# Two grouped-query attention blocks: scores computed transposed, exponentials written straight as P^T, sums by a ones-matmul, and one order by hand that mixes attention with the projections

## The chip, the cores and the metric

The kernel runs on one core of one Trainium2 chip. The metric is device microseconds of one launch. The engines are TensorE (PE, with its weight loads shown as PEld), VectorE (DVE), ScalarE (ACT), GpSimd (POOL) and the DMA queues, of which SyncE's (SP) is the main one here. Matrices are bf16, accumulation in PSUM is fp32.

## The reference

Two independent problems, A and B, of the same shape; the outputs stand side by side.

```
x [16, 32, 1024]   k_cache, v_cache [16, 4, 512, 128]   wq [1024, 4096]   wo [4096, 1024]
q = x @ wq                       -> [16 batches, 32 heads, 32 rows, 128]
k, v: each of the 4 kv heads serves 8 query heads
p = softmax(q k^T / sqrt(128))   -> rows of 512
o = p v
out = o (heads joined) @ wo      -> [16, 32, 1024];  concatenate A and B on the last axis
```

A *group* below is one batch and one kv head: 8 heads x 32 rows = 256 query rows against 512 keys. There are 64 groups in a problem and 128 in all.

## The kernel before

Everything is laid out so that the contracted index lies on the 128 partitions. x is transposed on TensorE (L123) into `xT`. `q_projection` makes 32 heads per problem, each 8 matmuls of 512 columns (L145), evacuated with the scale 1/sqrt(128) on ACT (L92) and DVE (L97) by turns. `attention` then walks over batches and kv heads. For one group:

- two matmuls of 512 columns give the scores, query rows on the partitions (L189, `s_ps`);
- DVE takes the negated row maximum (L197, `nmx`), ACT the exponential of each half with that bias, which also accumulates the row sums (L203, `p_sb`, `rs`);
- DVE inverts the sums (L211), POOL multiplies the probabilities by them (L214);
- eight 128x128 transposes on TensorE turn P into P^T (L222, `pT_ps`), and DVE copies it to SBUF (L228, `pT`);
- four matmuls of 256 columns with V as weights give the output (L231, `o_ps`), and ACT copies it into `oT` (L238).

`o_projection` makes 32 tiles of 128x256 per problem, each 32 matmuls of 256 columns (L254, `f_ps`), evacuates them (L90, L95) and sends them out (L264). K arrives by a transposing DMA of 1 MB per two batches (L170, `kT`, two buffers), V by 512 KB per batch (L178, three buffers), wq in 512 KB and wo in 2 MB pieces (L139, L248). All of them are issued from SP's queue, so a transfer that waits for its buffer holds back those behind it.

The order of instructions on each engine is set by the framework's scheduler from the priorities of the program's order, with a few order-only links; it puts B's q projection into A's attention, and most of A's output projection into B's attention.

Of the kernel before, what the change touches and what calls it, by code (L numbers as in the profile page):

```python
# [9 lines left out]
FP32 = mybir.dt.float32  # L11
ACTF = mybir.ActivationFunctionType
# [3 lines left out]
P = 128  # L16
# [5 lines left out]
SCALE = float(DH) ** -0.5  # L22


@with_exitstack
def kernel(
# [16 lines left out]
    _, _, SK, _ = A_k_cache.shape  # L43
# [5 lines left out]
    WH = 2  # L49
    OCW = 256  # L50
    NOC = NOUT // OCW
    KB = 2

    out_flat = out.flatten_outer_dims()

    const = ctx.enter_context(tc.tile_pool(name="const", bufs=1))
    xpool = ctx.enter_context(tc.tile_pool(name="xpool", bufs=1))
    wqpool = ctx.enter_context(tc.tile_pool(name="wqpool", bufs=6))
    wopool = ctx.enter_context(tc.tile_pool(name="wopool", bufs=2))
    qopool = ctx.enter_context(tc.tile_pool(name="qopool", bufs=3))  # L60
    ktpool = ctx.enter_context(tc.tile_pool(name="ktpool", bufs=2))
    vpool = ctx.enter_context(tc.tile_pool(name="vpool", bufs=3))
    work = ctx.enter_context(tc.tile_pool(name="work", bufs=3))
    small = ctx.enter_context(tc.tile_pool(name="small", bufs=4))
    outpool = ctx.enter_context(tc.tile_pool(name="outpool", bufs=3))
    psum = ctx.enter_context(
        tc.tile_pool(name="psum", bufs=1, space=bass.MemoryType.PSUM)
    )

    ident = const.tile([P, P], BF16, name="ident")  # L70
    make_identity(nc, ident[:])

# [5 lines left out]
    ORDER_ONLY = mybir.DependencyInfo(mybir.DependencyClass.NoSync, mybir.DependencyReason.DATA)  # L78

    def after(inst, first, why):  # L80
        if first is not None and inst is not None:
            tc.add_manual_dep(inst.ins, first.ins.name, ORDER_ONLY, reason=why)

    evac_toggle = [0]

    def _evac(out_ap, in_ap, scale):
        evac_toggle[0] ^= 1
        if evac_toggle[0]:
            if scale is None:
                nc.scalar.copy(out=out_ap, in_=in_ap)  # L90
            else:
                nc.scalar.mul(out=out_ap, in_=in_ap, mul=scale)  # L92
        else:
            if scale is None:
                nc.vector.tensor_copy(out=out_ap, in_=in_ap)  # L95
            else:
                nc.vector.tensor_scalar_mul(out=out_ap, in0=in_ap, scalar1=scale)  # L97
# [215 lines left out]
```

## Time and profile before

| | |
|---|---|
| median of 3 runs | 436.87 us (436.11 to 437.38) |
| span of the profiled execution, first to last instruction | 433.9 us (the page gives no other time of its own; the median is 2.97 us above this span) |
| TensorE busy | 418.8 us, 97% of the span, granted clock 1.00 |
| VectorE busy | 279.5 us, 64% |
| ScalarE busy | 256.4 us, 59% |
| GpSimd busy | 176.4 us, 41% |
| DMA | 71.89 MB, SP's queue at 74.8% of 16 engines' time |

Read it by stages: up to about 70 us there is q projection of A alone, to about 208 us attention of A with q projection of B, then a short stretch of q projection, to about 355 us attention of B with output projection of A, and then output projection alone. A busy share is an average over these. A row of instructions gives the count, the busy time of their union and the mean length of one; since matmuls overlap in the array, the mean length is a latency, and the pace comes from counts in a window of one kind of work. Some matmul records are missing from the trace (494 of 512 of the q projection are there).

### The profile page before, as it was taken

Reading aid. Unit: us, or ns where it says so; the run is one execution under the profiler, and the core shown is the slowest. Engines: PE = TensorE matmul, PEld = TensorE weight load, DVE = VectorE, ACT = ScalarE, POOL = GpSimd, SP = SyncE. Lnnn points to the kernel's source line nnn. Section 1 sums busy time; section 2 is a strip of 40 time slices with the busy share of each in tenths; the row PEclk is TensorE's granted clock in tenths of the full one; section 3 lists DMA queues with packets and bytes.
Section 4 is the critical chain, followed back from the end, with each engine's and each line's share of the span. In section 5 each row is a group of like instructions: output and inputs, shape, how many; then the busy total and the mean of one; then the engine's idle time right before and its main releaser. Section 6 shows DMA issues by size and latency. Waiting matters only on the chain.

```text
span 433.9 us, 8980 instructions
## 1 busy us (share of the span) xinstructions
PE 418.8 (97%) x3343; PEld 280.7 (65%) x3392; DVE 279.5 (64%) x564; ACT 256.4 (59%) x693; POOL 176.4 (41%) x262
## 2 busy tenths in 40 slices
PE   3999999999999999999999999999999999999997
PEld 2544444665666666566566766667667678888886
DVE  0122214999999999999269999999999950000000
ACT  2121113888888888888259888998988850000000
POOL 0000001566666666666126666666666640000000
PEclk9999999999999999999999999999999999999999
DMA  8945699797596999995566595995579007458800
GB/s 273 261 144 145 163 257 272 177 201 166 137 234 134 158 207 269 221 185 108 130 173 109 120 184 118 268 204 111 122 165 274 12 8 185 137 132 211 213 20 18
DMA packets 204076, 71.89 MB, mean 166 GB/s; under 512 B 133376, under 2 KB 203008, under 8 KB 204032
## 3 DMA queue, kind: packets, MB, share of 16 engines
q1 hardware_dynamic: 204032, 71.31, 74.8%
q8 instruction: 26, 0.43, 0.4%
q14 instruction: 18, 0.15, 0.1%
HBM read 52.43 MB, written 2.10 MB: 126 GB/s over the span
## 4 chain that ended last, share of the span: by engine, by line
PE 90%; DVE 3%; issue 2%; POOL 2%; DMA 1%; SPq 1%; DVEq 0%; POOLq 0%
PE f_ps L254 26%; PE q_ps L145 25%; PE pT_ps L222 16%; PE o_ps L231 14%; PE s_ps L189 10%; POOL p_sb L214 2%; DMA wq_sb<-in_A_wq_dram 1%; DVE nmx L197 1%; SPq L111 1%; DVE pT L228 1%; PE xT_ps L123 1%; DVE qT L97 0%; DVE rr L211 0%; DVE o_sb L95 0%; DVEq L95 0%
## 5 line engine op out<-in xcount | busy, mean ns | idle before, releaser
L214 POOL TENSOR_SCALAR p_sb<-p_sb,rr 128x512 bf16<-128x512 bf16 x256 | 175.7, 692 | 177.2 <-DVE rr L211 126.5
L203 ACT ACTIVATE p_sb<-s_ps,nmx 128x512 bf16<-128x512 f32 x256 | 173.9, 685 | 27.8 <-DVE nmx L197 12.4
L197 DVE TENSOR_REDUCE nmx<-s_ps 128x2 f32<-128x1024 f32 x128 | 154.4, 1207 | 0.5 <-PE s_ps L189 0.5
L254 PE MATMUL f_ps<-wo_sb,oT 128*128 128x256 bf16 x1024 | 123.1, 273 | 1.0
L254 PEld LDWEIGHTS <-oT 128*128 128x128 bf16 x1024 | 99.9, 98 | 24.3
L228 DVE COPY pT<-pT_ps 128x1024 bf16<-128x1024 bf16 x128 | 88.3, 690 | 12.2 <-PE pT_ps L222 4.9
L222 PE MATMUL pT_ps<-ident,p_sb 128*128 128x128 bf16 x1024 | 93.2, 220 | 1.9 <-POOL p_sb L214 0.6
L145 PEld LDWEIGHTS <-wq_sb 128*128 128x128 bf16 x512 | 50.0, 99 | 60.7 <-DMA wq_sb<-in_A_wq_dram 2.2
L222 PEld LDWEIGHTS <-p_sb 128*128 128x128 bf16 x1024 | 68.0, 98 | 21.8 <-POOL p_sb L214 14.1
L231 PE MATMUL o_ps<-pT,v_sb 128*128 128x256 bf16 x512 | 77.3, 273 | 0.2
L189 PE MATMUL s_ps<-kT,qT 128*128 128x512 bf16 x225 | 69.1, 379 | 0.3 <-ACT p_sb L203 0.2
L145 PE MATMUL q_ps<-xT_b,wq_sb 128*128 128x512 bf16 x244 | 63.9, 379 | 1.2
L231 PEld LDWEIGHTS <-v_sb 128*128 128x128 bf16 x512 | 43.1, 97 | 33.4 <-DVE pT L228 18.6
L145 PE MATMUL q_ps<-xT,wq_sb 128*128 128x512 bf16 x250 | 57.3, 387 | 2.3 <-DMA wq_sb<-in_A_wq_dram 2.0
L238 ACT CAST oT<-o_ps 128x256 bf16<-128x256 f32 x128 | 47.8, 373 | 15.2 <-PE o_ps L231 11.5
L97 DVE TENSOR_SCALAR qT<-q_ps 128x512 bf16<-128x512 f32 x32 | 22.1, 689 | 52.6 <-PE q_ps L145 52.6
L95 DVE CAST o_sb<-f_ps 128x256 bf16<-128x256 f32 x16 | 6.8, 422 | 70.9 <-PE f_ps L254 70.9
L92 ACT ACTIVATE qT<-q_ps 128x512 bf16<-128x512 f32 x32 | 19.1, 596 | 54.7 <-PE q_ps L145 51.9
L203 ACT ACTIVATION_READ_ACCUMULATOR p_sb<-s_ps,nmx 128x1 f32 x256 | 50.9, 199 | 0.0
L90 ACT CAST o_sb<-f_ps 128x256 bf16<-128x256 f32 x16 | 5.9, 371 | 66.8 <-PE f_ps L254 66.8
L211 DVE RECIPROCAL rr<-rs 128x1 f32<-128x1 f32 x256 | 36.6, 153 | 2.1 <-ACT p_sb L203 2.0
L189 PEld LDWEIGHTS <-qT 128*128 128x128 bf16 x256 | 20.1, 98 | 2.2 <-issue 0.9
(13 smaller groups left out, 21.0 us busy)
## 6 DMA issues: line engine op xcount, KB each, us to landing
wq_sb<-in_A_wq_dram SPq DMA_DIRECT2D x16, 512.0 KB, 4.2
v_sb<-in_A_v_cache_dram SPq DMA_DIRECT2D x16, 512.0 KB, 5.1
wq_sb<-in_B_wq_dram SPq DMA_DIRECT2D x16, 512.0 KB, 5.4
wo_sb<-in_A_wo_dram SPq DMA_DIRECT2D x4, 2048.0 KB, 9.7
v_sb<-in_B_v_cache_dram SPq DMA_DIRECT2D x16, 512.0 KB, 4.1
wo_sb<-in_B_wo_dram SPq DMA_DIRECT2D x4, 2048.0 KB, 9.3
out_dram<-o_sb SPq DMA_DIRECT2D x32, 64.0 KB, 2.3
x_sb<-in_A_x_dram SPq DMA_DIRECT2D x4, 256.0 KB, 3.2
```

Of the source, the lines that this page charges most:

```text
L97: nc.vector.tensor_scalar_mul(out=out_ap, in0=in_ap, scalar1=scale)
L145: nc.tensor.matmul(q_ps[:], lhsT=wq_sb[:, dc, hl * DH:(hl + 1) * DH], rhs=xT[:, dc, :], start=(dc == 0), stop=(dc == DC - 1),)
L189: sm = nc.tensor.matmul(s_ps[:, half, :], lhsT=qT[:, b, h0:h0 + HALF, :].rearrange("p h s -> p (h s)"), rhs=kT[:, bl, g, :], start=True, s ...
L197: nc.vector.tensor_reduce(out=nmx[:], in_=s_ps[:], axis=AX.X, op=ALU.max, negate=True)
L203: nc.scalar.activation(out=p_sb[:, half, :], in_=s_ps[:, half, :], func=ACTF.Exp, bias=nmx[:, half:half + 1], scale=1.0, accum_out=rs[:, h ...
L211: rc = nc.vector.reciprocal(out=rr[:, half:half + 1], in_=rs[:, half:half + 1])
L214: nc.gpsimd.tensor_scalar(out=pn[:, half, :], in0=p_sb[:, half, :], scalar1=rr[:, half:half + 1], scalar2=1.0, op0=ALU.mult, op1=ALU.mult,)
L222: nc.tensor.transpose(pT_ps[:, kc, half * P:(half + 1) * P], pn[:, half, kc * P:(kc + 1) * P], ident[:],)
L228: prev_pT_evac = nc.vector.tensor_copy(out=pT[:], in_=pT_ps[:])
L231: nc.tensor.matmul(o_ps[:], lhsT=v_sb[:, g, kc, :], rhs=pT[:, kc, :], start=(kc == 0), stop=(kc == KC - 1),)
L238: nc.scalar.copy(out=oT[:, g * REP:(g + 1) * REP, b * SQ:(b + 1) * SQ], in_=o_ps[:].rearrange("p (h s) -> p h s", s=SQ),)
L254: nc.tensor.matmul(f_ps[:], lhsT=oT[:, h, tt * P:(tt + 1) * P], rhs=wo_sb[:, h, :], start=(h == 0), stop=(h == HQ - 1),)
```

## The change

The whole program is rewritten in one function, `fast_path`, with a hand-written order (no scheduler), and a second function, `general_path`, that holds a plain version of the kernel before and is entered only behind a branch.

- **Transposed scores.** K^T is the weight and q the moving operand: for each group four matmuls of 256 columns give the scores with the keys on the partitions (`scores`, L350). The keys are taken with a step of 4 in K^T, so that partition p of piece c holds key 4p+c, and V is loaded to match, which makes its rows in a partition consecutive.
- **Exponential straight to P^T.** One ACT instruction of 1024 columns with a fixed shift of 44 and the scale (L358). No maximum, no transposes, no copy of P^T.
- **Sums.** DVE adds the four pieces in two instructions (L366, L370); a matmul of a 128x128 matrix of one constant (2^-75) with that sum, both operands `float32r`, puts the total on all partitions (L389). ACT takes the logarithm (L397) and the exponential of its negative (L401); DVE multiplies the unnormalized output by it (L415).
- **Range check.** One row of the logarithms of four groups goes by a DMA from POOL's queue into `lall` (L404); at the end DVE counts the entries within 20 in magnitude, a matmul sums the counts, and all five engines read the count and branch (L528, L530): if an entry is out of range the general path computes everything again.
- **Order.** All projection matmuls form one stream of 1024 units (512 columns each; the output projection is now in tiles of 512 columns). 64 units of A's q projection run first; then each of 128 slots holds the scores of group i, 4 units, the values and sum of group i-1, 3 units; the last 64 units follow. A's groups run kv head by kv head, so that attention can begin after 8 heads.
- **Loads.** K and V come per four groups (512 KB each, two buffers), in A as four transposing DMAs of 128 KB (L274), in B as one of 512 KB (L277). wq and wo come in 1 MB pieces (L250, L259) into a pool of 20 buffers, at slots that a table gives. x of B is transposed by a DMA (L482). The first piece of wq is issued from ACT's queue. Outputs leave from POOL's queue (L325), the last from SP's.
- **Start.** Eight matmuls on zeros run before the first transposes; the ACT table that holds both functions is loaded once.

The order on VectorE for two groups of the first attention, before (`nmx`, `rr`, `pT` belong to a group, `qT` is a head's evacuation):

```order
L197 TENSOR_REDUCE nmx<-s_ps 128x2
L211 RECIPROCAL rr<-rs 128x1
L228 COPY pT<-pT_ps 128x1024
L211 RECIPROCAL rr<-rs 128x1
L197 TENSOR_REDUCE nmx<-s_ps 128x2
L211 RECIPROCAL rr<-rs 128x1
L228 COPY pT<-pT_ps 128x1024
L211 RECIPROCAL rr<-rs 128x1
L197 TENSOR_REDUCE nmx<-s_ps 128x2
L97 TENSOR_SCALAR qT<-q_ps 128x16x32
```

and now, two slots of A's attention (`t_572` is the first sum of the four pieces, `t` the second):

```order
L366 TENSOR_TENSOR t_572<-p_sb 128x512
L370 TENSOR_TENSOR t<-t_572 128x256
L415 SCALAR_TENSOR_TENSOR oT<-r,ob 128x8x32
L305 CAST qT<-q_ps 128x16x32
L366 TENSOR_TENSOR t_603<-p_sb 128x512
L370 TENSOR_TENSOR t<-t_603 128x256
L415 SCALAR_TENSOR_TENSOR oT<-r,ob 128x8x32
L305 CAST qT<-q_ps 128x16x32
```

The maximum, the inverses and the copy of P^T are gone; two additions and the final product stand in their place, and every q evacuation is now here. On TensorE, the end of a group's transposes before:

```order
L222 LDWEIGHTS p_sb
L222 MATMUL pT_ps<-ident,p_sb 128x128
L189 LDWEIGHTS qT
L189 MATMUL s_ps<-kT,qT 128x512
L189 LDWEIGHTS qT
```

and now the end of a group's values, its sum, and the next unit:

```order
L382 LDWEIGHTS v_sb
L382 MATMUL ob<-p_sb,v_sb 128x256
L389 MATMUL ob<-t,ones 128x256
L297 LDWEIGHTS wq_sb
L297 MATMUL q_ps<-xT,wq_sb 128x512
```

The sum's matmul has no weight-load instruction of its own in front. On SP's queue, where B's wo is loaded during B's attention:

```order
L277 DMA_TRANSPOSE kT<-in_B_k_cache_dram 128x4x512
L280 DMA v_sb<-in_B_v_cache_dram 128x4x512
L259 DMA wo_sb<-in_B_wo_dram 128x8x512
L277 DMA_TRANSPOSE kT<-in_B_k_cache_dram 128x4x512
L280 DMA v_sb<-in_B_v_cache_dram 128x4x512
L259 DMA wo_sb<-in_B_wo_dram 128x8x512 x3
L277 DMA_TRANSPOSE kT<-in_B_k_cache_dram 128x4x512
L280 DMA v_sb<-in_B_v_cache_dram 128x4x512
```

where before one 2 MB piece stood between K and V loads:

```order
L170 DMA_TRANSPOSE kT<-in_B_k_cache_dram 128x8x512
L178 DMA v_sb<-in_B_v_cache_dram 128x16x128
L248 DMA wo_sb<-in_A_wo_dram 128x32x256
L264 DMA out_dram<-o_sb 128x256
```

The core of the diff, the new function cut to the parts that the prediction speaks of:

```diff
-                nc.vector.tensor_reduce(
-                    out=nmx[:], in_=s_ps[:], axis=AX.X, op=ALU.max, negate=True
-                )
...
-                        nc.tensor.transpose(
-                            pT_ps[:, kc, half * P:(half + 1) * P],
-                            pn[:, half, kc * P:(kc + 1) * P],
-                            ident[:],
-                        )
...
+            def scores(i):
+                pr, b, g = where(i)
+                kT = kv_tiles[i // GRP][0].rearrange("p q (k c) -> p q c k", c=KC)
+                s_ps = psum.tile([P, KC, QW], FP32, name="s_ps", tag="s")
+                for c in range(KC):
+                    nc.tensor.matmul(
+                        s_ps[:, c, :],
+                        lhsT=kT[:, i % GRP, c, :],
+                        rhs=qT[pr, g][:, b, :, :].rearrange("p h s -> p (h s)"),
+                        start=True, stop=True,
+                    )
+                p_sb = work.tile([P, KC, QW], BF16, name="p_sb", bufs=3)
+                nc.scalar.activation(
+                    out=p_sb[:], in_=s_ps[:], func=ACTF.Exp, bias=shift[:], scale=SCALE)
...
+            def partial_sums(i):
+                t1 = work.tile([P, 2, QW], FP32, name="t1")
+                nc.vector.tensor_tensor(
+                    out=t1[:], in0=p_sb[:, 0:2, :], in1=p_sb[:, 2:4, :], op=ALU.add)
+                t = work.tile([P, QW], FP32R, name="t")
+                nc.vector.tensor_tensor(
+                    out=t[:], in0=t1[:, 0, :], in1=t1[:, 1, :], op=ALU.add)
...
+            def values(i):
+                ob = psum.tile([P, 2 * QW], FP32, name="ob", tag="ob")
+                for c in range(KC):
+                    nc.tensor.matmul(ob[:, 0:QW], lhsT=v_sb[:, i % GRP, c, :],
+                                     rhs=d["p"][:, c, :], start=(c == 0), stop=(c == KC - 1))
+                nc.tensor.matmul(
+                    ob[:, QW:2 * QW], lhsT=ones[:], rhs=d["t"][:], start=True, stop=True)
+                nc.scalar.activation(out=lg[:, q, :], in_=ob[:, QW:2 * QW], func=ACTF.Ln)
+                nc.scalar.activation(out=r[:], in_=lg[:, q, :], func=ACTF.Exp, scale=-1.0)
+                if q == GRP - 1:
+                    nc.gpsimd.dma_start(out=lall[j:j + 1, :], in_=lg[0:1, :, :]...)
+            def normalize(i):
+                nc.vector.scalar_tensor_tensor(out=oT[pr, tt][...], in0=d["r"][:]...,
+                    scalar=ONES, in1=d["ob"][:, 0:QW]..., op0=ALU.mult, op1=ALU.mult)
...
+            for j in range(2, 2 * NG // GRP):
+                at(max(0, GRP * (j - 2) + 1), load_kv, j)
+            for c4 in range(3, 16):
+                need = (c4 - 2) * 4 * DC / 7.0
+                at(max(0, int(need) - 10), load_wq, c4 // 8, c4 % 8)
+            at(12, load_xT_b)
+            for nh in range(NH):
+                for hg in range(HKV):
+                    at(NG - 12 + nh * 8 + hg * 2, load_wo, 0, nh, hg)
+                    at(NG + 20 + nh * 18 + hg, load_wo, 1, nh, hg)
...
+            for i in range(2 * NG):
+                do_loads(i)
+                scores(i)
+                run(units, 4)
+                if i > 0:
+                    values(i - 1)
+                partial_sums(i)
+                run(units, 3)
+                if i > 0:
+                    normalize(i - 1)
...
+    ok = nc.values_load(ok_i[0:1, 0:1], min_val=0, max_val=total, ...)
+    with tc.If(ok < total, preferred_fallthrough_block=False):
+        general_path(tc, problems, out_flat)
```

More of the change, by code (lines that the diff above doesn't have):

```diff
@@ L76 @@
     ]
[L78 to L97, printed above, removed]
@@ L278 @@
[L278 to L282 removed]
+                p_sb = work.tile([P, KC, QW], BF16, name="p_sb", bufs=3)
+                nc.scalar.activation(
+                    out=p_sb[:], in_=s_ps[:], func=ACTF.Exp, bias=shift[:], scale=SCALE
+                )
```

549 lines of the change are left out of this document (373 added, 176 removed).

## The prediction

> **What bounds the kernel now.** I read the engines' shares first, then the chain that ended last, then stretches of one kind of work, and last the groups and single rows.
>
> ```profile
> span 433.9 us, 8980 instructions
> PE 418.8 (97%) x3343; PEld 280.7 (65%) x3392; DVE 279.5 (64%) x564; ACT 256.4 (59%) x693; POOL 176.4 (41%) x262
> PE 90%; DVE 3%; issue 2%; POOL 2%; DMA 1%; SPq 1%; DVEq 0%; POOLq 0%
> 30.00:40.00 10.00, 9.95 (x47) 4.52 (x47) 1.77 (x3) 1.79 (x3) 0.00 (x0) 1.00 0.55 157
> 140.00:160.00 20.00, 19.61 (x159) 12.33 (x162) 19.54 (x42) 17.42 (x50) 13.09 (x20) 1.00 1.07 179
> 280.00:300.00 20.00, 19.76 (x182) 14.04 (x185) 19.14 (x40) 17.78 (x50) 13.78 (x20) 1.00 0.76 156
> 394.00:404.00 10.00, 10.00 (x94) 8.96 (x92) 0.85 (x2) 0.37 (x1) 0.00 (x0) 1.00 0.49 123
> ```
>
> TensorE carries 90% of the chain. The windows' columns are busy time and count of PE, weight loads, DVE, ACT and POOL, then clock, DMA share and GB/s. In the attention windows DVE is busy 19.54 and 19.14 us of 20, so there both engines are full, and taking work from TensorE alone would give nothing; the change takes work from both.
>
> The pace of a matmul comes from the last window, output projection alone: 94 of 256 columns in 10.00 us, **0.1064 us each**. For 512 columns I take twice that, **0.2128 us**; 49 recorded ones in 10.74 us with 494 of 512 on record (rows below) give 0.2115, so no fixed cost per instruction shows.
>
> ```profile
> L222 PE MATMUL pT_ps<-ident,p_sb 128*128 128x128 bf16 x1024 | 93.2, 220 | 1.9 <-POOL p_sb L214 0.6
> L254 PE MATMUL f_ps<-wo_sb,oT 128*128 128x256 bf16 x1024 | 123.1, 273 | 1.0
> L231 PE MATMUL o_ps<-pT,v_sb 128*128 128x256 bf16 x512 | 77.3, 273 | 0.2
> L145 PE MATMUL q_ps<-xT_b,wq_sb 128*128 128x512 bf16 x244 | 63.9, 379 | 1.2
> L145 PE MATMUL q_ps<-xT,wq_sb 128*128 128x512 bf16 x250 | 57.3, 387 | 2.3 <-DMA wq_sb<-in_A_wq_dram 2.0
> 23.44 10.74 PE q_ps L145 x49
> 10.75 1.03 PE L145 MATMUL q_ps<-xT,wq_sb 128*128 128x512 bf16 x2 [1.97 <-DMA wq_sb<-in_A_wq_dram]
> 12.43 7.88 PE L145 MATMUL q_ps<-xT,wq_sb 128*128 128x512 bf16 x29
> 424.77 6.17 PE L254 MATMUL f_ps<-wo_sb,oT 128*128 128x256 bf16 x55
> 431.04 0.42 DVE L95 CAST o_sb<-f_ps 128x256 bf16<-128x256 f32 x1 [6.56 <-PE f_ps L254]
> out_dram<-o_sb SPq DMA_DIRECT2D x32, 64.0 KB, 2.3
> ```
>
> TensorE streams from 10.75 us (first q matmul) to 424.77 + 6.17 = 430.94: 420.2 us. The matmuls of 512 columns are 512 (q) and 256 (scores), those of 256 columns 1024 (output projection) and 512 (values): 768 x 0.2128 + 1536 x 0.1064 = 326.9 us. The **remaining 93.3 us** are the 1024 transposes of P, some 40 of x, a slow start and all gaps.
>
> **The change part by part.** The sum is made against the span of 433.9; the runs' median is 436.87, so I add 3.0 at the end.
>
> *Projections, scores, values: 0.* The same columns stream through the array, only cut otherwise (output projection 512 of 512 columns, scores 512 of 256): 326.9 us again. The weight of the scores is now read with a step of 4 elements. Nothing in this trace reads a weight with a step. Below: 0, a load stays hidden behind its matmul. Above: a load takes twice the 98 ns of the row below, and as nothing then hides 90 ns of it, 512 x 0.09 = 46 us. I take 0, since every load row, whatever its operand, is 97 to 99 ns, and keep the other end for a rival.
>
> *Transposes, gaps, slow start: -93.3*, and back come the items below.
>
> *The sum's matmul: +32.* 128 of 256 columns, float32r. No fp32 matmul is in this trace. Lower bound: a bf16 matmul of that width with its load hidden, 0.106. Upper bound: four passes, each with a load that nothing hides, 4 x (0.106 + 0.098) = 0.82.
>
> ```profile
> L231 PEld LDWEIGHTS <-v_sb 128*128 128x128 bf16 x512 | 43.1, 97 | 33.4 <-DVE pT L228 18.6
> L254 PEld LDWEIGHTS <-oT 128*128 128x128 bf16 x1024 | 99.9, 98 | 24.3
> ```
>
> The instruction has no load of its own ahead of it, so I expect the load exposed, once for two-byte or twice for four-byte weights: 0.106 + 0.098 to 0.196 = 0.20 to 0.30. I take 0.25: 128 x 0.25 = 32.0. The Trainium skill, in "FP8 and Floating Point Precision", section "TensorE Precision Notes", says that true fp32 goes through the array in four passes, and lists a reduced form that reads four bytes and truncates. By four passes this term would be an estimated 55 us in place of 32; by one pass with a hidden load 14. No row here can tell which form float32r is.
>
> *Gaps that stay: +4.5.* The attention windows show 0.24 to 0.39 us of TensorE idle in 20, 1.2 to 2%. A slot is 7 x 0.2128 + 8 x 0.1064 + 0.25 = 2.59 us, 128 of them 332 us; 1.3% of that.
>
> For gaps to stay this small, ACT and DVE must fit in 2.59 us, and their chain must be ahead of TensorE's use:
>
> ```profile
> L203 ACT ACTIVATE p_sb<-s_ps,nmx 128x512 bf16<-128x512 f32 x256 | 173.9, 685 | 27.8 <-DVE nmx L197 12.4
> L238 ACT CAST oT<-o_ps 128x256 bf16<-128x256 f32 x128 | 47.8, 373 | 15.2 <-PE o_ps L231 11.5
> L92 ACT ACTIVATE qT<-q_ps 128x512 bf16<-128x512 f32 x32 | 19.1, 596 | 54.7 <-PE q_ps L145 51.9
> L97 DVE TENSOR_SCALAR qT<-q_ps 128x512 bf16<-128x512 f32 x32 | 22.1, 689 | 52.6 <-PE q_ps L145 52.6
> L95 DVE CAST o_sb<-f_ps 128x256 bf16<-128x256 f32 x16 | 6.8, 422 | 70.9 <-PE f_ps L254 70.9
> ```
>
> ACT: 256 more columns cost 596 - 373 = 223 ns, so 1024 columns of exp cost 685 + 446 = 1.13 us; logarithm and second exp 0.37 each: 1.88 us, 73% of a slot. The function tables are loaded once, so no reload is in it. DVE: additions of 512 and 256 columns like the rows of those widths, 0.69 and 0.42, the product 0.42, and 7/8 of a q evacuation 0.60: 2.13 us, 82%; with output projection units only 0.15 for evacuation, 1.68. So both fit. In time: scores end 0.43 into a slot, exp at 1.75, the additions at 2.86; TensorE wants that exp and that sum in the next slot at 2.59 + 1.28 and 2.59 + 1.70. Slack is 1.4 us for the sum. The queue behind a late addition is DVE's product and q evacuation, for which `ob` and `q_ps` have two buffers each. POOL's multiply (692 ns, 256 times) has no successor on any engine; its loss is free.
>
> *Loads: +3.* A K transpose of 1 MB holds SP for 4.6 to 8.6 us and lands in 8.3; so 512 KB cost about 2.3 to 4.3 of SP and 4.2 to landing, a V piece 4.5 alone, 1 MB of wo half of 9.4.
>
> ```profile
> L170 SPq DMA_TRANSPOSE kT<-in_A_k_cache_dram x8: 4649/6029/8644, 50.4 to 169.1; - x8
> DMA to landing us min/median/max: 6.8/8.3/11.2
> DMA to landing us min/median/max: 3.9/4.5/11.1
> DMA to landing us min/median/max: 9.1/9.4/12.4
> ```
>
> (The three landing rows are K, V, wo.) K of four groups may be fetched from the last scores of the buffer's old owner to its first use, 4.8 slots or 12.4 us, V about as long. Per four slots (10.4 us) the queue moves K, V and 0.9 MB of wq: 4.2 + 2.2 (half of V's landing taken as its share) + 4.1 = 10.5. That is tight but was so before: DMA share 1.07 at 140 to 160. V's rows are now 1 KB instead of 256 bytes, wq's 1 KB instead of 512, so I count it as covered. Uncovered is B's wo: three 1 MB pieces follow V at slots 88 and 104. From V's release in the middle of slot 88 or 104 on, 2.2 + 3 x 4.7 = 16.3 us are 6.3 slots, and K's 4.2 us another 1.6: K of slots 96 and 112 lands about half a slot after it is wanted, and the last wo piece of the second burst, behind another V, up to two slots. That is up to 7 us in all; the wider rows should take some of it, and I take 3 (0 to 7).
>
> *Start: +1.* The first q matmul waited for wq at 10.75, behind both x; now wq comes through a second queue while x of A is in flight, the same 2 MB in all: 0. The first 29 q matmuls took 7.88 us where 6.2 is the pace; the eight warm-up matmuls may cure that; I leave 1 of it.
>
> *End: +2.* The last evacuation is 512 columns on DVE (0.69 for 0.42), the last piece out is 128 KB, after which the engines branch twice. The program's own start holds a branch, and ACT idles there 0.73 us:
>
> ```profile
> 0.73 1.28 ACT L90 ACT_TABLE_LOAD   x1 [0.73 <-PEq L297]
> ```
>
> Two such are 1.5, with 0.27 and some for the piece 2. The Trainium skill, in "Runtime: NRT & Kernel Launch", section "Instruction fetch mechanics", speaks against it: a taken branch to code outside the window being fetched must wait for that page. It gives no time; the skipped general path is far larger than a page, so that wait would lie in this term, behind the landing of the last piece or not.
>
> **Sum:** 433.9 - 93.3 + 32.0 + 4.5 + 3 + 1 + 2 = 383.1; with 3.0 outside the span **386 us**.
>
> **The rivals.**
>
> - *Cheap sum.* The float32r matmul runs as a bf16 one: 0.106 x 128 = 13.6, so 386 - 18 = 368. For it: all loads in this trace hide. Against: no separate load instruction.
> - *Four passes, loads hidden.* 4 x 0.106 = 0.43 each, 55: 386 + 23 = 409. For it: operands are four bytes wide.
> - *A hand-over sets the slot, or the stepped load does.* If ACT and DVE, each some 80% full, wait for each other so that a slot needs 2.9 us, that is 0.3 x 128 = 38: 424; with the stepped loads exposed 432. For it: now, too, DVE is full and yet PE shows gaps. Against: the slack worked out above, and two buffers everywhere.
> - *Slower: the sum's matmul with four exposed loads.* 0.82 each, 105 in place of 32: 386 + 73 = 459. Place: the end of every slot's values on TensorE, where nothing overlaps it. It decides from (433.9 - 351.1) / 128 = 0.65 us per matmul on. For it: four bytes, no load of its own. Against: it needs every unknown at its worst.
> - *Slower: K feeds too slowly.* A's four transposes of 128 KB per four slots: if each cost SP 3.5 us, 14 us plus 0.8 for V and wq stand against 10.4, 16 times: +70. For it: four times as many issues. Against: by proportion 0.6 to 1.1 each.
> - *The fast path is not the whole run.* If the branch is taken, all is computed again, some 400 us more. The logarithm is that of 512 exponentials of small scores times 2^-75 e^44: 6.2 - 52 + 44 = -1.8, far within 20.
>
> **How the numbers follow.** Forecast 40%, cheap sum 24%, four passes 16%, hand-over or stepped load 8%, sum at over 0.65 us 5%, slow K 5%, branch 1%, other 1%. A difference under 0.3% (1.3 us) cannot be told from none. Faster: 40 + 24 + 16 and 7 of the 8 = 87%; slower: 5 + 5 + 1 = 11%; same: the 2% left. The range takes in the cheap sum with fewer gaps, 362, and four passes with late loads, 418; both slower cases lie outside.
>
> **What would show it.** TensorE at 97% or more of the attention with slots of 2.6 us; the L389 row at a pace of 0.2 to 0.3 us beyond its neighbours; ACT at 73% and DVE at about 80% in A's attention; no wait on `kT` but one or two of a few us near slots 96 and 112; the wo row to landing under 5 us. I am wrong if L389's gap is under 0.15 or over 0.4, if TensorE waits for DVE or ACT in every slot, if the scores' loads are longer than 98 ns, or if the end after the last matmul exceeds 6 us.

## The result, and the profile after

The change takes 373.04 us (median of 4 runs, 371.70 to 374.23) against 436.5 us for the kernel before on the same chip: ratio 0.8546, 95% interval 0.8521 to 0.8571, so 63 us less. The profiled execution took 374.23 us with a span of 372.5.

Of the profile after: the span and the engines' shares, the chain that ended last by engine and by line, and two groups of instructions (busy time, mean ns of one, idle time before them and its cause).

```profile
span 372.5 us, 6012 instructions
PE 357.2 (96%) x2176; PEld 224.3 (60%) x2218; DVE 243.5 (65%) x476; ACT 248.9 (67%) x387; POOL 25.1 (7%) x53
PE 94%; DMA 3%; issue 1%; DVE 1%; SPq 0%
PE q_ps L297 30%; PE f_ps L314 30%; PE s_ps L350 15%; PE ob L382 15%; PE ob L389 4%; DMA x_sb<-in_A_x_dram 2%; DMA v_sb<-in_A_v_cache_dram 1%; SPq L428 0%; PE xT_ps L444 0%; DVE xT L448 0%; DVE qT L305 0%; DVE o_sb L323 0%; PE ok_ps L520 0%
L350 PEld LDWEIGHTS <-kT 128*128 128x128 bf16 x512 | 56.6, 114 | 29.5 <-issue 1.0
L389 PEld LDWEIGHTS ob<-t,ones 128*128 128x128 f32 x128 | 24.3, 190 | 1.4
```

On the chain DVE falls from 3% to 1% and POOL from 2% to nothing: TensorE's matmuls are 94% of it. The windows of the two attentions, columns as in the prediction:

```profile
76.00:126.00 50.00, 49.65 (x314) 32.26 (x318) 39.83 (x77) 38.01 (x60) 2.44 (x5) 1.00 0.85 214
280.00:330.00 50.00, 49.65 (x314) 32.29 (x319) 32.25 (x65) 38.13 (x60) 5.32 (x10) 1.00 0.72 200
```

TensorE is 99.3% busy. DVE is at 80% with q evacuations and 65% with output projection, ACT at 76%: where DVE was busy 19.54 us of 20 before, no engine beside TensorE is full now. One slot on TensorE, from the timeline:

```profile
100.19 0.60 PE L350 MATMUL s_ps<-qT,kT 128*128 128x256 bf16 x4
100.63 1.03 PE L297 MATMUL q_ps<-xT,wq_sb 128*128 128x512 bf16 x4
101.49 0.60 PE L382 MATMUL ob<-p_sb,v_sb 128*128 128x256 bf16 x4
101.85 0.36 PE L389 MATMUL ob<-t,ones 128*128 128x256 f32 x1
102.28 0.59 PE L297 MATMUL q_ps<-xT,wq_sb 128*128 128x512 bf16 x2
102.71 0.60 PE L350 MATMUL s_ps<-qT,kT 128*128 128x256 bf16 x4
```

No row bears a wait. (In such a row matmuls overlap: it ends one latency, 0.273 us for 256 columns and 0.379 for 512, after its last matmul started.) From scores to scores is 102.71 - 100.19 = 2.52 us. (Of the three units behind the sum two are on record; the time of the third is there.) The two ends of the run, from the timeline and from SP's semaphore rows (mean durations, then from when to when):

```profile
10.42 4.00 PE L297 MATMUL q_ps<-xT,wq_sb 128*128 128x512 bf16 x9 [0.88 <-DVE xT L448]
27.69 0.60 PE L350 MATMUL s_ps<-qT,kT 128*128 128x256 bf16 x4 [0.78 <-DVE qT L305]
357.37 7.08 PE L314 MATMUL f_ps<-wo_sb,oT 128*128 128x512 bf16 x31
364.48 0.69 DVE L323 CAST o_sb<-f_ps 128x512 bf16<-128x512 f32 x1 [6.39 <-PE f_ps L314]
365.20 0.36 SPq L325 DMA_DIRECT2D out_dram<-o_sb  x1
```

```profile
L530 SPq EVENT_SEMAPHORE  x8: 17/17/17, 366.3 to 368.1; - x8
L557 SPq EVENT_SEMAPHORE  x14: 17/28/28, 370.8 to 372.4; - x14
```

Matmuls end at 364.45, and the program 8.05 us later; before it was 433.9 - 430.94 = 3.0.

### The profile page after: what moved, and what is told of

Same layout as the page of the kernel before. It is cut to its first block, busy times and chain, and to the rows that moved or that the text cites. A ratio compares the mean times of both kernels' runs of the same rounds, so it can differ in the third digit from the quotient of the medians.

```text
span 372.5 us, 6012 instructions
## 1 busy us (share of the span) xinstructions
PE 357.2 (96%) x2176; PEld 224.3 (60%) x2218; DVE 243.5 (65%) x476; ACT 248.9 (67%) x387; POOL 25.1 (7%) x53
## 4 chain that ended last, share of the span: by engine, by line
PE 94%; DMA 3%; issue 1%; DVE 1%; SPq 0%
PE q_ps L297 30%; PE f_ps L314 30%; PE s_ps L350 15%; PE ob L382 15%; PE ob L389 4%; DMA x_sb<-in_A_x_dram 2%; DMA v_sb<-in_A_v_cache_dram 1%; SPq L428 0%; PE xT_ps L444 0%; DVE xT L448 0%; DVE qT L305 0%; DVE o_sb L323 0%; PE ok_ps L520 0%
## 5 line engine op out<-in xcount | busy, mean ns | idle before, releaser
L358 ACT ACTIVATE p_sb<-s_ps,shift 128x1024 bf16<-128x1024 f32 x128 | 142.6, 1114 | 53.3 <-PE s_ps L350 53.3
L297 PE MATMUL q_ps<-xT,wq_sb 128*128 128x512 bf16 x491 | 130.8, 386 | 2.0 <-DVE xT L448 0.9
L314 PE MATMUL f_ps<-wo_sb,oT 128*128 128x512 bf16 x491 | 129.0, 380 | 1.0
L350 PE MATMUL s_ps<-qT,kT 128*128 128x256 bf16 x512 | 76.8, 273 | 1.2 <-DVE qT L305 0.8
L382 PE MATMUL ob<-p_sb,v_sb 128*128 128x256 bf16 x512 | 76.8, 273 | 0.1
L397 ACT ACTIVATE lg<-ob 128x256 f32<-128x256 f32 x128 | 49.3, 385 | 39.8 <-PE ob L389 39.8
L350 PEld LDWEIGHTS <-kT 128*128 128x128 bf16 x512 | 56.6, 114 | 29.5 <-issue 1.0
L314 PEld LDWEIGHTS <-oT 128*128 128x128 bf16 x512 | 44.7, 98 | 33.0
L401 ACT ACTIVATE r<-lg 128x256 f32<-128x256 f32 x128 | 53.7, 420 | 4.1
L415 DVE SCALAR_TENSOR_TENSOR oT<-r,ob 128x256 bf16<-128x256 f32 x128 | 53.4, 417 | 1.1 <-ACT r L401 1.1
L389 PE MATMUL ob<-t,ones 128*128 128x256 f32 x128 | 46.4, 362 | 0.0
L404 POOL DMA_DIRECT2D lall<-lg x32 | 15.9, 496 | 251.0 <-ACT lg L397 251.0
L389 PEld LDWEIGHTS ob<-t,ones 128*128 128x128 f32 x128 | 24.3, 190 | 1.4
L325 POOL DMA_DIRECT2D out_dram<-o_sb x15 | 8.6, 571 | 82.2 <-DVE o_sb L323 76.3
```

The costliest lines, as they stand in the source:

```text
L297: nc.tensor.matmul(ps[:], lhsT=w[:, dc, (h % 4) * DH:(h % 4 + 1) * DH], rhs=xT[pr][:, dc, :], start=(dc == 0), stop=(dc == DC - 1),)
L314: nc.tensor.matmul(ps[:], lhsT=oT[pr, tt][:, h, :], rhs=wo_tiles[pr, nh, h // REP][:, h % REP, :], start=(h == 0), stop=(h == HQ - 1),)
L350: nc.tensor.matmul(s_ps[:, c, :], lhsT=kT[:, i % GRP, c, :], rhs=qT[pr, g][:, b, :, :].rearrange("p h s -> p (h s)"), start=True, stop=True,)
L358: nc.scalar.activation(out=p_sb[:], in_=s_ps[:], func=ACTF.Exp, bias=shift[:], scale=SCALE)
L382: nc.tensor.matmul(ob[:, 0:QW], lhsT=v_sb[:, i % GRP, c, :], rhs=d["p"][:, c, :], start=(c == 0), stop=(c == KC - 1),)
L389: nc.tensor.matmul(ob[:, QW:2 * QW], lhsT=ones[:], rhs=d["t"][:], start=True, stop=True)
```

## Experiments

Short diffs are against the changed kernel, or against the kernel before where it says so. The experiments ask four things: what the sum's matmul costs, what the transposes cost and whether DVE or TensorE held the kernel before, whether the order by hand is what keeps TensorE full, and where the two ends go.

### The sum's matmul

```diff
-            ones = const.tile([P, P], FP32R, name="ones")
+            ones = const.tile([P, P], BF16, name="ones")
...
-                t = work.tile([P, QW], FP32R, name="t")
+                t = work.tile([P, QW], BF16, name="t")
```

> The sum's matmul takes bf16 operands (the constant matrix and DVE's last sum) instead of float32r; nothing else changes. In the trace of the changed kernel a slot lasts 2.517 us where 7 x 0.2128 + 8 x 0.1064 = 2.341 stand without the sum, so the float32r matmul costs about 0.18 us, 0.07 more than a bf16 matmul of 256 columns. Theory (the extra 0.07 is its exposed four-byte weight load): slot 2.45 us, time 373 - 128 x 0.07 = 364 us. Rival 1 (the 0.07 is a gap at the end of every slot, whatever the type): 373 us. Rival 2 (float32r streams its columns at a slower rate and the load hides): also 364 us, so this run does not part it from the theory; the length of the weight-load row does.

Measured: 370.18 us, ratio to before 0.8463 (0.8435 to 0.8492). Two neighbouring slots and the load's group:

```profile
100.60 0.60 PE L350 MATMUL s_ps<-qT,kT 128*128 128x256 bf16 x4
103.09 0.60 PE L350 MATMUL s_ps<-qT,kT 128*128 128x256 bf16 x4
...
L389 PEld LDWEIGHTS <-ones 128*128 128x128 bf16 x128 | 12.5, 98 | 1.5
```

The slot is 2.49 us, 0.03 less, and the whole run 2.9 us less. The theory of an exposed load fell here: it asked for 0.07 us per slot and 364 us. The slot without the sum is 2.382 us by the paces worked out further below, so the bf16 matmul leaves 0.108, the pace of any of 256 columns, and the float32r one 0.138.

The second experiment issues the same float32r matmul twice:

```diff
                 nc.tensor.matmul(ob[:, QW:2 * QW], lhsT=ones[:], rhs=d["t"][:], ...)
+                nc.tensor.matmul(ob[:, QW:2 * QW], lhsT=ones[:], rhs=d["t"][:], ...)
```

> The sum's matmul is issued twice in a row in every slot, to the same place with the same result. Theory (each costs 0.18 us on TensorE, which sets the slot): +128 x 0.18 = +23 us, 396 us. Rival (what costs is the change between types, not the matmul: the second one then costs only its columns, 0.107): +14 us, 387 us. Were TensorE not the bound of a slot: under +5 us.

Measured: 389.31 us, 0.8918 (0.8892 to 0.8944).

```profile
102.93 0.60 PE L350 MATMUL s_ps<-qT,kT 128*128 128x256 bf16 x4
105.57 0.60 PE L350 MATMUL s_ps<-qT,kT 128*128 128x256 bf16 x4
```

The slot is 2.64 us, so the second one costs 0.12, and 16.3 us / 128 = 0.127 by the times, nearer the rival's 0.107 than the theory's 0.18. Although its load row reads 190 ns, twice that of bf16, nearly all of it lies beside other matmuls. So one float32r matmul of 256 columns costs 0.12 to 0.14 us here, where bf16 takes 0.109: one pass. The Trainium skill, in "FP8 and Floating Point Precision", section "TensorE Precision Notes", lists a reduced form of fp32 that reads four bytes and truncates, beside a true one of four passes; the time fits the first, and four passes (0.44) are excluded for these operands.

### Was it the transposes, or VectorE?

First the array work of the transposes is put back into the changed kernel: eight matmuls of 128 columns with P as weights, written into a part of `ob` that the sum overwrites, with no copy by DVE.

```diff
+                for c in range(KC):
+                    for half in range(2):
+                        nc.tensor.matmul(ob[:, QW + half * P:QW + (half + 1) * P],
+                            lhsT=d["p"][:, c, half * P:(half + 1) * P], rhs=ident[:], ...)
```

> Eight matmuls of 128 columns against the identity, with the 128x128 blocks of the exponentials as weights, are put back in front of the sum's matmul in every slot; their result is overwritten. That is the array work of the old transposes without their place in the chain. The prediction priced 1024 transposes, all gaps and a slow start together at 93.3 us and did not part them. Theory A (the transposes themselves cost about 0.08 us each, bound by load and columns together): +82 us, 455 us. Theory B (they cost their 128 columns, 0.053 us, and a third of the 93.3 us were gaps at the hand-overs of the old chain): +55 us, 428 us.

Measured: 437.19 us, 1.0003 (0.9984 to 1.0022): the whole gain is gone.

```profile
100.88 0.60 PE L350 MATMUL s_ps<-qT,kT 128*128 128x256 bf16 x4
...
102.61 0.61 PE L391 MATMUL ob<-ident,p_sb 128*128 128x128 bf16 x8
...
103.89 0.60 PE L350 MATMUL s_ps<-qT,kT 128*128 128x256 bf16 x4
...
L391 PE MATMUL ob<-ident,p_sb 128*128 128x128 bf16 x1024 | 78.1, 219 | 0.0
```

The slot is 3.01 us, 0.49 more, and the run 64 us longer, between the two expectations. The eight matmuls themselves account for most of it: their row is 0.61 us long and one lasts 0.219, so they follow each other every (0.61 - 0.219) / 7 = 0.056 us, 0.45 in a slot and 57 us in the run. That is near the second theory's 0.053. The other 0.04 to 0.05 us of a slot come in with the sum's matmul, which now stands behind matmuls of 128 columns and no longer behind matmuls of 256; that its load of 190 ns is then hidden less would fit, but no run tests it.

The old transposes show what the kernel before lost besides. Its 1024 have a busy time of 93.2 us (row L222 in the prediction), the same number here 78.1. The 15.1 us more are pauses inside the rows of transposes. They are shorter than a matmul's latency of 0.22 us, so the page counts them as busy and not as waits. The gain is thus the array time of the transposes, 57 us; what the closed gaps give back is about what the sum's matmul, the start and the end cost (terms below).

Next, in the kernel before, DVE's part alone: no row maximum, a constant bias of zero.

```diff
-                nc.vector.tensor_reduce(
-                    out=nmx[:], in_=s_ps[:], axis=AX.X, op=ALU.max, negate=True)
...
```

> The kernel before, without the row maximum: the bias of the exponential is a constant zero (the inputs are small; for large ones the result would overflow). TensorE's work is unchanged, DVE loses 128 x 1.207 us. The transposes put back cost 0.062 us each, so of what TensorE spent beyond its 512- and 256-column matmuls in the kernel before some 20 us are neither transposes nor start. Theory (that is waiting for the hand-overs through a full DVE): 437 falls by 10 to 20 us. Rival (TensorE alone sets the time, the 20 us are its own, such as the change between kinds of matmul): 437 stays within 3 us.

Measured: 428.53 us, 0.9815 (0.9783 to 0.9847), 7.8 us less, between the theory's 10 to 20 and the rival's 3. A window of its first attention and the row of its transposes:

```profile
140.00:160.00 20.00, 19.95 (x175) 12.47 (x173) 11.67 (x34) 18.93 (x56) 14.62 (x22) 1.00 1.08 247
...
L220 PE MATMUL pT_ps<-ident,p_sb 128*128 128x128 bf16 x1024 | 78.8, 219 | 0.8 <-POOL p_sb L212 0.7
```

DVE falls from 19.54 to 11.67 us of 20, TensorE has hardly any gap left (19.95), and the transposes' busy time falls from 93.2 to 78.8 us: the pauses inside them go with the row maximum. All that is worth only 8 us. ACT stands at 18.93 and would be next.

Then TensorE's part alone, again in the kernel before: of eight transposes per group one stays, and the rest of P^T is a constant, written once.

```diff
+                        if half < 1 or kc < KC - 1:
+                            continue
                         nc.tensor.transpose(pT_ps[:, kc, half * P:(half + 1) * P], ...)
...
```

> The kernel before with one transpose of eight: seven of the eight blocks of P^T that DVE copies are constants, so the output is not the reference's; maximum, exponentials, normalization and the copy of all of P^T stay. TensorE loses 896 transposes, 56 us at 0.062. Theory of the prediction (DVE is full in the attention windows, 19.1 to 19.5 us of 20, so work taken from TensorE alone gives nothing but the gaps): 437 falls by under 12 us. Rival (TensorE alone is the bound): -56 us, 381 us.

Measured: 386.55 us, 0.8852 (0.8823 to 0.8882), 50 us less. A window of its second attention and the row of its scores (durations, then from when to when):

```profile
260.00:280.00 20.00, 19.93 (x163) 14.56 (x161) 19.96 (x44) 18.55 (x55) 13.80 (x21) 1.00 0.94 189
...
L193 PE MATMUL s_ps<-kT,qT x256: 376/379/379, 71.2 to 331.8; 128*128 128x512 bf16 x128
```

and, of the kernel before, the same row and the two rows of its timeline between which no scores run:

```profile
L189 PE MATMUL s_ps<-kT,qT x225: 376/379/379, 70.5 to 349.0; 128*128 128x512 bf16 x113
...
202.00 0.59 PE L189 MATMUL s_ps<-kT,qT 128*128 128x512 bf16 x2
...
220.11 1.03 PE L189 MATMUL s_ps<-kT,qT 128*128 128x512 bf16 x4
```

DVE is full in that window (19.96), as it was; by the prediction nothing should have come of it. The 50 us come from elsewhere. Attention ends 17 us earlier (331.8 for 349.0), since the stretch without any scores between the two attentions (202.0 to 220.1, its last 10 us q projection alone) is gone, and the tail of output projection alone shrinks from 433.9 - 349.0 = 84.9 to 384.2 - 331.8 = 52.4 us: projection matmuls moved into the TensorE time that the transposes left. The 50 us are also 896 x 0.056. (The copy of P^T now also waits for one transpose instead of eight; what that alone is worth no run tells.) Leaving out the 16 us by which that stretch is longer than a usual group, a group takes (349.0 - 70.5 - 16) / 127 = 2.07 us before and (331.8 - 71.2) / 127 = 2.05 here. So inside the attentions DVE does hold the pace, as the prediction says; but over the whole kernel TensorE's total set the time, and DVE's full windows were worth only the 8 us of the run without a maximum, in which the stretch without scores grew to 34 us (184.7 to 218.4).

### The order and the stepped weights

Values and sums of a group in the slot of its own scores, not one slot later:

```diff
                 scores(i)
                 run(units, 4)
-                if i > 0:
-                    values(i - 1)
                 partial_sums(i)
+                values(i)
                 run(units, 3)
-                if i > 0:
-                    normalize(i - 1)
-            run(units, 4)
-            values(2 * NG - 1)
-            run(units, 4)
-            normalize(2 * NG - 1)
+                normalize(i)
+            run(units, 8)
```

> The changed kernel with the values and the sum of group i in its own slot, behind 4 units, instead of one slot later; all work is the same. In the trace the scores' start to the exponential's end is 1.77 us and the two sums end 0.70 + 0.42 later. TensorE reaches the values 1.30 us after the scores' start and the sum 0.44 later. Theory (the hand-written order of one slot's distance is what hides ACT and DVE): TensorE waits 0.5 us for the exponential and then until 2.9 us for the sum, so a slot takes 2.52 + 1.2 = 3.7 us: 373 + 128 x 1.2 = 525 us (500 to 545). Rival (the queues' depth lets the later units pass, or two buffers suffice): below 400 us.

Measured: 550.68 us, 1.2595 (1.2550 to 1.2639), a little above the expected range. One slot of the first attention on its timeline:

```profile
199.83 0.60 PE L350 MATMUL s_ps<-qT,kT 128*128 128x256 bf16 x4
...
201.33 0.69 DVE L305 CAST qT<-q_ps 128x512 bf16<-128x512 f32 x1 [0.68 <-PE q_ps L297]
201.63 0.60 PE L382 MATMUL ob<-p_sb,v_sb 128*128 128x256 bf16 x4 [0.34 <-ACT p_sb L358]
201.94 0.68 DVE L366 TENSOR_TENSOR t<-p_sb 128x512 f32<-128x512 bf16 x1
203.14 0.38 PE L389 MATMUL ob<-t,ones 128*128 128x256 f32 x1 [0.91 <-DVE t L370]
204.02 0.60 PE L350 MATMUL s_ps<-qT,kT 128*128 128x256 bf16 x4
```

This slot is 4.19 us (the mean is 2.52 + 178 / 128 = 3.91). TensorE waits first for the exponential (0.34), then for the additions (0.91). The additions stand behind a q evacuation in DVE's queue: the exponential is there by 201.63, the evacuation runs until 201.33 + 0.69 = 202.02. That is what the expectation had missed. The one-slot delay is worth 178 us, more than any other part that a run takes out. Without it the same removal of work would have made a slower kernel.

K taken without a step of four in the weights (the probabilities then meet other rows of V):

```diff
-                kT = kv_tiles[i // GRP][0].rearrange("p q (k c) -> p q c k", c=KC)
+                kT = kv_tiles[i // GRP][0].rearrange("p q (c k) -> p q c k", c=KC)
```

> The changed kernel with K^T taken as weight in consecutive columns instead of with a step of 4; V stays as it is, so keys and values do not match and the output is not the reference's. The weight load of K^T lasts 113 ns with the step against 98 for all others. Theory (it hides behind the 256-column matmul): no change within 1 us, and the load row falls to 98 ns. Rival (part of it is exposed): up to 512 x 0.015 = 8 us faster.

Measured: 374.27 us, 0.8563 (0.8533 to 0.8594), no difference that the intervals show; the rival's 8 us are excluded.

```profile
L350 PEld LDWEIGHTS <-kT 128*128 128x128 bf16 x512 | 50.0, 98 | 34.3 <-issue 1.1 <-DMA kT<-in_B_k_cache_dram 0.4
```

The load with a step takes 114 ns instead of 98, and stays hidden.

### The two ends

No range check and no branch; only the fast path stays:

```diff
-    ok = nc.values_load(ok_i[0:1, 0:1], min_val=0, max_val=total, ...)
-    with tc.If(ok < total, preferred_fallthrough_block=False):
-        general_path(tc, problems, out_flat)
```

> The reading of the count into registers, the branch and the general path are left out (the count itself is still made; inputs out of range would no longer be computed by the general path). After the last matmul the changed kernel's span goes on for 8.0 us against 3.0 before. Theory (each engine's jump over the skipped general path waits for its instructions to be fetched; SP jumps only after the last piece of output has landed, 368.1, and goes on at 370.8): the span loses 2.7 us and the 0.6 us of reading that stands ahead of SP's wait hides behind the landing, so -3 us, 370 us. Rival (the tail is the larger last piece and its landing): no change within 1 us.

Measured: 369.82 us, 0.8469 (0.8445 to 0.8493), 3.2 us less. Its end:

```profile
span 368.1 us, 6024 instructions
...
364.52 0.69 DVE L323 CAST o_sb<-f_ps 128x512 bf16<-128x512 f32 x1 [6.39 <-PE f_ps L314]
365.24 0.36 SPq L325 DMA_DIRECT2D out_dram<-o_sb  x1
```

The last evacuation stands where it did; from it to the end is 3.6 us instead of 8.0 (by the medians the gain is 3.2, near the expected 3). With the branch, SP's last wait at L530 ends at 368.1 when the piece has landed, and its first instruction past the skipped block is at 370.8 (rows above). Those 2.7 us are paid behind the landing. The Trainium skill, in "Runtime: NRT & Kernel Launch", section "Instruction fetch mechanics", says that a taken branch out of the fetched window stalls for the page; the trace agrees, and 2.7 us is its price here. Between 368 and 371 us the DMA queues of kind instruction move 3 packets; in the run without the branch they move none from 357 us to the end. The other 1.7 us by which the two traces differ are not the jump: the last piece lands 2.8 us after its issue with the branch and 1.9 without, and the semaphores behind the jump (L557) run on for 1.6 us. Why the landing differs is not shown.

All outputs from POOL's queue, so that SP may jump before the last piece is out:

```diff
-                        (nc.sync if last else nc.gpsimd).dma_start(
+                        nc.gpsimd.dma_start(
```

> The changed kernel with its last piece of output issued from POOL's queue like the others, so that SP, which in its branch waits only for transfers of its own kind, need not wait for the last piece before it jumps. Theory (SP's 2.7 us of jumping then runs beside the landing): the landing is 3.7 us from POOL against 2.8 from SP and its issue 0.57 against 0.36, so the span loses 2.7 - 0.9 - 0.2 = 1.6 us: 371.5 us. Rival (POOL itself must still read the count and jump behind that issue, and its jump takes as long): 373 us or more.

Measured: 371.78 us (369.85 to 373.84), 0.8510 (0.8480 to 0.8541).

```profile
L530 SPq EVENT_SEMAPHORE  x8: 17/17/17, 357.7 to 358.2; - x8
L557 SPq EVENT_SEMAPHORE  x14: 17/28/28, 361.1 to 370.1; - x14
```

SP now jumps at 358.2 and is past it at 361.1, beside the last matmuls. From the last matmul to the end is 6.7 us in place of 8.05, 1.35 less; the other engines still jump after their last work. The intervals of the two times overlap, so the gain is seen in the trace, and the medians alone don't show it.

At the start, between the pieces of x, matmuls on zeros that fill TensorE's pauses:

```diff
+                for _ in range((2, 3, 1, 4)[tt]):
+                    nc.tensor.matmul(warm_ps[:], lhsT=warm[:, 0:P], rhs=warm[:], ...)
```

> The changed kernel with 2, 3, 1 and 4 more matmuls of 512 columns on zeros behind the transposes of the four tiles of x, where TensorE waits for the next tile. In the changed kernel's trace the eight warm-up matmuls end at 4.8 us, TensorE then idles 2.7 us in pieces until 10.42, the granted clock is 0.50 from 9 to 15 us, and the first 64 q matmuls take 16.3 us where 13.8 is the pace. Theory (the pauses before 10.42 let the clock fall back): the clock stays up and 1.5 to 2.5 us go, less up to 0.5 by which the first q matmul may be later: 371 to 372 us. Rival (matmuls on zeros do not keep the clock up, or its fall has another cause): 373 us or more.

Measured: 371.19 us, 0.8502 (0.8487 to 0.8517). After's windows at the start, then this kernel's:

```profile
9.00:12.00 3.00, 2.12 (x10) 0.87 (x8) 0.69 (x1) 0.35 (x1) 0.00 (x0) 0.50 1.18 332
12.00:15.00 3.00, 2.78 (x7) 1.06 (x7) 0.69 (x1) 0.00 (x0) 0.00 (x0) 0.50 0.89 192
```

```profile
9.00:12.00 3.00, 2.99 (x18) 1.30 (x16) 0.69 (x1) 0.40 (x1) 0.00 (x0) 1.00 1.20 325
...
10.14 13.97 PE L297 MATMUL q_ps<-xT,wq_sb 128*128 128x512 bf16 x64
```

The granted clock is 0.50 in the changed kernel from 9 to 15 us, and 1.00 with the pauses filled; the first 64 units take 13.97 us instead of 27.69 - 0.78 - 10.42 = 16.49 (the 0.78 is the wait in front of the first scores, which both kernels have). The stretch differs from run to run: the window from 12 to 15 us shows 0.54 in the run without a branch and 0.83 in that with the bf16 sum, whose starts are the same as the change's. That fits the spread of the four runs of the change, 2.5 us, against 0.7 us in the five runs here. Between the warm-up and the first unit stand both pauses and transposes; which of them lets the clock fall is not taken apart.

The eight warm-up matmuls taken away altogether:

```diff
-            for _ in range(8):
-                nc.tensor.matmul(warm_ps[:], lhsT=warm[:, 0:P], rhs=warm[:], ...)
...
```

> The changed kernel without the eight warm-up matmuls. Theory (they end 5.6 us before the first q matmul and are lost again): within 1 us of 373. Rival (they shorten the slow stretch, which would else last for some 8 more matmuls of 0.43 us): +1.5 to +2 us.

Measured: 374.25 us, 0.8563 (0.8544 to 0.8582). The medians differ by 1.2 us, and the intervals overlap, so alone the eight gain nothing that can be told from none.

```profile
12.00:15.00 3.00, 3.00 (x8) 1.03 (x7) 0.54 (x1) 0.00 (x0) 0.00 (x0) 1.00 0.95 185
...
10.85 16.52 PE L295 MATMUL q_ps<-xT,wq_sb 128*128 128x512 bf16 x64 [0.88 <-DVE xT L441]
```

The first 64 units take 16.52 us without the eight and 16.49 with them.

### The parts together

The bf16 sum, the filled pauses and the last output from POOL in one kernel, range check included:

```diff
-            ones = const.tile([P, P], FP32R, name="ones")
+            ones = const.tile([P, P], BF16, name="ones")
...
+                for _ in range((2, 3, 1, 4)[tt]):
...
-                        (nc.sync if last else nc.gpsimd).dma_start(
+                        nc.gpsimd.dma_start(
```

> The changed kernel with three edits together: bf16 operands of the sum's matmul (measured alone: -2.9 us), the matmuls on zeros between x's transposes, and the last piece from POOL's queue. Theory (each stands at another place of TensorE's time, so they add): -2.9 - 2.0 - 1.6 = -6.5, 366.5 us. If only the first holds: 370 us.

Measured: 366.73 us (366.56 to 366.86), ratio to before 0.8396 (0.8382 to 0.8410), and outside the change's interval: the best of these kernels. Alone the three gave -2.86, -1.85 and -1.26 us, -6.0 in all, and together -6.3: the parts add up, with the last of them within the noise when it stands alone.

No run here takes apart the new loads (V's wider rows, the 1 MB pieces, x of B by a DMA), the inverse by logarithm and exponential, or the multiply that POOL lost.

## Why the prediction came out, step by step

The direction, the engine that sets the time and the shares of ACT and DVE (76 and 80% for 73 and 82) were right, and the time, 373.04, lies 13 us under the 386 forecast and inside the range. The terms, against the span of before:

| term | predicted | measured | from |
|---|---|---|---|
| transposes, gaps, slow start | -93.3 | -87.0 | pace of after |
| projections, scores, values | 0 | -0.8 | 1024 x 0.2155 + 1024 x 0.1092 = 332.5 for 333.2 |
| the sum's matmul | +32.0 | +17.7 | slot, 128 x 0.138 |
| gaps that stay | +4.5 | 0 | timeline |
| loads | +3 | 0 | no wait of PE on `kT`, `v_sb`, `wo_sb` |
| start | +1 | +3.2 | timeline |
| end | +2 | +5.05 | timeline |
| between slots and tail | 0 | +0.4 | remainder |
| span | 383.1 | 372.5 | |
| outside the span | +3.0 | +1.7 | 374.23 - 372.5 |

That the total is only 13 us off is in part luck. The terms taken too high come to 24 us (the sum's matmul 14.3, gaps 4.5, loads 3, outside the span 1.3, cutting 0.8), those taken too low to 12 us (transposes and gaps 6.3, end 3.05, start 2.2, remainder 0.4), and half of the error cancelled. The last 1.2 us lie between the profiled run, the slowest of four, and the median.

**The pace.** "94 of 256 columns in 10.00 us" gave 0.1064; the step that failed is taking a window's count for a rate, since matmuls that straddle its edges count whole. The row of 55 in 6.17 us, which the prediction quotes for the end, gives (6.17 - 0.273) / 54 = 0.1092. The same way 512 columns take 0.2155: the row of 64 in 13.97 us gives (13.97 - 0.379) / 63 = 0.2157, seven in a row of 1.67 us 0.215. The prediction's second reading, 0.2115, came out low since it spread the missing records evenly; its own row alone gives (10.74 - 0.379) / 48 = 0.2159. Then the matmuls that stay are 768 x 0.2155 + 1536 x 0.1092 = 333.2, and 420.2 - 333.2 = 87.0 remained: 57.3 for 1024 transposes at 0.056, an estimated 2.2 for the 40 of x, 1.6 of slow start (7.88 - 29 x 0.2155), and by difference 25.9 of gaps. Of these, 15.1 are the pauses inside the rows of transposes; for the rest no run gives a place. The busy share of 97% hid most of them.

**"So I expect the load exposed".** This is the term that was mis-sized most, by 14 us. The slot of 2.52 less 7 x 0.2155 + 8 x 0.1092 = 2.382 leaves 0.138. A matmul without its own load instruction in the listing still has one on the load row (190 ns), and most of it runs beside the matmuls ahead of it. The rival of a cheap sum (368) was nearer than the forecast. By the prediction's own mark, a gap "under 0.15" means that this step was wrong.

**"Both engines are full, and taking work from TensorE alone would give nothing".** It gives 50 us, by the run with one transpose. The reading of the windows was right, and the step from them to the whole kernel failed: DVE was full only where attention ran, and the projections, half of TensorE's time (512 x 0.2155 + 1024 x 0.1092 = 222 of 420 us), had room to move. The forecast did not suffer, since the change takes work from both.

**Gaps and loads.** (1.3% of 332 is 4.3; the prediction has 4.5.) Slack of 1.4 us was enough for no gap in a slot, since with the bf16 sum the slot is its matmuls and nothing more; the rival of a hand-over chain has nothing for it. TensorE's waits in the whole run are 4.9 us, all of it up to the first scores. The four largest (in total, times, longest us):

```profile
PE xT_ps L444 <- DMA x_sb<-in_A_x_dram: 1.8, 3, 0.8
PE warm_ps L437 <- DVE warm L224: 1.2, 1, 1.2
PE q_ps L297 <- DVE xT L448: 0.9, 1, 0.9
PE s_ps L350 <- DVE qT L305: 0.8, 1, 0.8
```

On loads the prediction expected waits near slots 96 and 112 and wo landing "under 5 us". There was none, although the pieces landed later than that (KB each, median from issue to landing):

```profile
wo_sb<-in_B_wo_dram SPq DMA_DIRECT2D x8, 1024.0 KB, 7.8
```

So the landing was mis-sized and its cover under-rated. The chain that ended last does list 1% for a V piece, from 172.36 us on; on the timeline TensorE's rows run through that moment without a wait. A chain is inferred from the last releaser; where a row of it has no idle time beside it on the engine, it cost nothing.

**The stepped weights** were to show 97 to 99 ns and showed 114, which the prediction had named as a sign that it is wrong; "stays hidden" held all the same, by the run without a step.

**The start.** "The eight warm-up matmuls may cure that" failed: what stands between them and the first unit, pauses and transposes, lets the clock fall again. The slow clock takes 16.49 - 64 x 0.2155 = 2.7 us of the first 64 units in the profiled run, and 0.78 is the first scores' wait for a q evacuation; the first unit began 0.33 earlier.

**The end.** The branch was priced by ACT's idle time at the program's start (0.73), which is a wait for a semaphore of TensorE's queue; no branch instruction is on record in the kernel before. The jump past the large block is 2.7 us on SP, behind the landing. "The end after the last matmul exceeds 6 us" came true, 8.05, and 2.7 us of it for the reason named there.

**Outside the span.** The 3.0 was a median of some runs less the span of another. One run's time less its own span is 1.7 in both kernels (436.25 - 434.5 before).

## What to carry to other kernels

Before calling an engine the bound from full windows, ask whether the other work of the busiest engine can move into the time that is freed: TensorE's total, not DVE's full attention windows, set this kernel's time. Here, with consumers one slot behind their producers and every other engine at 80% of a slot or less, TensorE ran without a gap; the same work in the same slot was 178 us slower. Take a pace from a contiguous row, its length less one latency over the count less one, and not from the count of a window. And compare the busy time of a group with the same work run without pauses: 15 us of waiting stood here inside an engine that was 97% busy.

## What the runs showed of the hardware

- A float32r matmul of 256 columns costs 0.12 to 0.14 us of TensorE's time against 0.109 for bf16; its load is 190 ns against 98 and nearly all hidden behind matmuls of 256 columns.
- A matmul of 128 columns with a fresh load for each follows the one ahead every 0.056 us, although its load row reads 98 ns; so the rows of loads are latencies as well.
- Eight matmuls on zeros ahead of the transposes of x do nothing measurable here; ten more between these transposes bring the granted clock from 0.50 to 1.00 and the first 64 units from 16.49 to 13.97 us. Without any, the units took 16.52 us, and 8 of them ran from 12 to 15 us where the pace is 14, while the clock column read 1.00 there: the column does not show that first slow stretch.
- A jump past a large skipped block takes SP 2.7 to 2.9 us; started before the last output it costs less of the end.
